# A gated mix of a 2-D FFT filter and a token MLP: 64-row matmul pairs for the odd residues' odd wavenumbers, and filter rows loaded among w2's tiles

## The chip, the cores and the metric

One core of one Trainium2 chip. The metric is the time of one execution on the device in microseconds; the median of several runs is taken.

## The reference, cut to what matters

```python
def _A_ref(x, w_r, w_i):                       # x: 1 x 2048 x 512, w: 2048 x 257
    X = rfft2(x.astype(float32), axes=(-2, -1))
    X = X * (w_r + 1j * w_i)
    return irfft2(X, s=(2048, 512), axes=(-2, -1)).astype(bfloat16)

def _B_ref(x, w1, b1, w2, b2):                 # w1: 2048 x 1792, w2: 1792 x 2048
    h = _layernorm(x, axis=-1)
    u = gelu(einsum("bsd,sf->bdf", h, w1) + b1)
    return (einsum("bdf,fs->bds", u, w2) + b2).transpose(0, 2, 1)

x = A_x
g = sigmoid((x * gate_w).sum(-1, keepdims=True))
return g * _A_ref(x, A_w_r, A_w_i) + (1 - g) * _B_ref(x, B_w1, B_b1, B_w2, B_b2)
```

All inputs are bfloat16. Branch A filters x with a 2-D Fourier transform; branch B is an MLP over the 2048 tokens; a gate per token mixes the two.

## The kernel before, in words

The 2048 tokens are read as 16 tiles `j` of 128 tokens, in four residues `r` modulo 4 and four quarters `q`. Residues are called even or odd below by `r`.

**Branch B** is matmuls of 128x128 weights on 512 columns. The first product (line L716) accumulates 16 token tiles into each of 14 feature tiles `ft`; ScalarE applies the gelu (L732) into `gl`. The second (L1065) accumulates the 14 feature tiles into each of the 16 token tiles; ScalarE scales and adds the bias (L1071). The weights of both products go through the same SBUF buffers: `wa` holds feature tiles 0 to 6, two `wb` buffers the rest, first w1's, then, when TensorE has done with them, w2's.

**Branch A** runs beside it, in stages:
- a radix-4 split over the quarters on VectorE (`q4a`, `q4b`), a DFT over tokens on TensorE (L565 to L568, table `ta`), evacuated by ScalarE (L571), and a second split (`d2`, `radix4`: L596 to L609). The spectrum lies in two halves `lt`: even wavenumbers (0) and odd ones (1). `sp0` and `sp1` (L621 to L639) repair one special column with twelve operations of a few elements;
- a DFT over the 512 channels (L664), evacuated by ScalarE (L671), recombined by `tb2` (L680 to L682, with twelve edge operations L686 to L688 in all) into `B`;
- the filter: a butterfly (`bfly`, L831, L832), products with the filter's real and imaginary part (`mul`, L839), their combination (`comb`, L844, L845) and a second butterfly (`ob`, L851 to L853), for `lt` 0 and then 1. Beside it stand the repairs of the first and last channel wavenumber, `wprep`, `c0a`, `c0b`, `c0c`, and of the Nyquist row, `nyq`, which works on one partition with 512 elements. Nine repaired lines are copied by DMA into `s9` (`lines`), multiplied by a small matrix on TensorE (`linem`, L871), copied out by ScalarE (L873) and written back into `B` by DMA;
- the inverse radix-4 split (`radix4` again) and the inverse DFT over tokens. For even residues it is `i1` (L929 to L934). For the odd residues' even wavenumbers it is `i1s` (L897): the 128 rows of contraction are two halves of 64 that share one table, so two 64-row matmuls run side by side, into banks `fa` and `fb`, and `eo2` (L905) adds and subtracts the halves. For the odd residues' odd wavenumbers it is `i1` with 256 columns (L925), evacuated by L940;
- `zf` and `fq` (L953 to L966), the inverse DFT over channels (`i3`, L1008 to L1012), evacuated with the gate as scale (L1016), then `es`, `es2` and `fin2` (L1042 to L1084) add branch A to branch B's tile. The last tile is finished by `fin` (L1078) in pieces.

**What sets the order.** Nothing is ordered on the chip. `add(engine, duration, emit, reads, writes, prio, ...)` records a task; `Plan.order` walks through a model of the five engines and the DMA with these durations, priorities and buffer counts, and the tasks are emitted in the order that results. Each engine then takes its instructions in that fixed order and waits on semaphores. The model's DMA has one queue, and `late` and `nbytes` of a load are its costs there.

**Loads.** All but a few go through SyncE's queue, in order: x and the first w1 tiles, the tables, the rest of w1, with the filter rows of `A_w_r` (`ld_W(0)`, 16 transfers) ahead of w1's last tiles and those of `A_w_i` (`ld_W(1)`, 16 transfers) behind them, then w2's 14 tiles with the inverse table `ti` and the channel table `tg` ahead of the last three. Filter rows have 257 elements, 514 bytes. SyncE has at most eight transfers under way.

The matmul of the odd residues' odd wavenumbers:

```python
for c in range(2):
    f = (5 - c) * P
    T.matmul(p1[:, v], lhsT=d(c), rhs=ti[:, f:f + L], start=(c == 0), stop=(c == 1))
```

Of the kernel before, what the change touches and what calls it, by code (L numbers as in the profile page):

```python
# [16 lines left out]
P = 128  # L17
# [13 lines left out]
def ti_at(r):  # L31
    return (0, 1024, 512, 1920)[r], (512, 896)[r % 2]


def make_tables():

    p = np.arange(P)
    r4 = np.arange(4)
# [6 lines left out]
    ti = np.zeros((P, 3072))  # L45
    for r in range(4):
# [6 lines left out]
        th = ang(s, 1 + 4 * (p ^ 96), S)  # L53
# [7 lines left out]
        if r % 2:  # L61
            sg = np.where(p < 64, 1.0, -1.0)[:, None]
            th = ang(k, s, S)
            v = v.reshape(P, 7, P)
            v[:, 0] = np.cos(th)
            v[:, 1] = sg * np.cos(th)
            v[:, 2] = -np.sin(th)
            v[:, 3] = -sg * np.sin(th)
            v[0, 2:4] = alt * (0.5 ** 0.5 if r == 1 else -(0.5 ** 0.5))
            th = ang(1 + 4 * (p ^ 96), s, S)  # L70
            v[:, 4] = -np.sin(th)
            v[:, 5] = np.cos(th)
            v[:, 6] = np.sin(th)
            ti[:, o:o + w] = v.reshape(P, w)
        else:
            s5 = np.append(s, 512)
            for lt, kk in enumerate((k, 1 + 4 * (p ^ 96))):
                th = ang(kk, s5, S)
                c, n = np.cos(th), -np.sin(th)
                if lt == 0:  # L80
                    n[0, 0:P] = 0.0 if r == 0 else -alt
                u = v[:, 256 * lt:256 * lt + 256]
                u[:, 0:P], u[:, P:] = c[:, 0:P], n[:, 0:P]
                if r == 0 and lt:
                    u[:, P] = -n[:, P]
                elif r == 0:
                    ti[:, 2816:2879], ti[:, 2943:3007] = n[:, 2:P:2], n[:, 1:P:2]
                    u[:, 0:65], u[:, 66:130] = c[:, 0:129:2], c[:, 1:P:2]
                    u[0, 66:130], ti[0, 2879:2943] = 0.0, 1.0
# [49 lines left out]
class Plan:  # L139
# [33 lines left out]
    def order(self):  # L173
# [17 lines left out]
        while events:  # L191
# [19 lines left out]
            while progress:  # L211
                progress = False
                for eng, ts in pending.items():
# [3 lines left out]
                    for t in ts:  # L217
                        if t.ready <= now + 1e-9 and all(caps[a] > 0 for a in t.alloc):
                            if best is None or key[t] < key[best]:
                                best = t  # L220
# [50 lines left out]
def kernel(  # L271
# [42 lines left out]
    def alloc_first():  # L314
# [15 lines left out]
        t["wn"] = sb([1, 2, WL], BF16, "wn")  # L330
# [3 lines left out]
        t["sp"] = sb([P, 4, 2, 4], F32, "sp")  # L334
# [3 lines left out]
        t["cm"] = sb([P, 4, 4, 2], F32, "cm")  # L338
# [94 lines left out]
    wsrc = (A_w_r, A_w_i)  # L433

    def ld_W(comp):
        v = wsrc[comp].rearrange("(e c k) l -> c e k l", e=4, k=4)
        z = wsrc[comp].rearrange("(v u w) l -> w u v l", v=4, u=2)

        def emit():
            W, u = t["W"][:, comp], t["wt"][:, comp]  # L440
            dma(u[64:127, :, 0:257], v[65:128, :, 0, :])
            dma(u[0:64, :, 0:257], v[64:128, :, 2, :])
            dma(u[127:128, 0:2, 0:257], z[0:1, 1, 2:4, :])
            dma(u[127:128, 3:1:-1, 0:257], z[0:1, 0, 0:4:3, :])
            for e in range(4):
                dma(W[:, 1, e, 1, 0:257], v[:, 3 - e, 3, :].rearrange("(o i) l -> o i l", o=4)[:, ::-1])
            for o in range(4):
                dma(W[32 * o:32 * o + 32, 1, :, 0, 0:257], v[96 - 32 * o:128 - 32 * o, :, 1, :])
            dma(W[1:64, 0, :, 0, 0:257], v[1:64, :, 0, :])
            dma(W[64:128, 0, :, 0, 0:257], v[0:64, :, 2, :])  # L450
            dma(W[0:1, 0, :, 0, 0:257].rearrange("w (u v) l -> w u v l", u=2), z[0:1, :, 0:2, :])
            dma(t["wn"][:, comp, 0:257], wsrc[comp][1024:1025, :])
        return emit

    for comp in range(2):
        add("SP", 12.3, ld_W(comp), writes=[("W", comp), ("wt", comp)], prio=17 + 8 * comp, nbytes=300000, after=[a0])
        if comp == 0:
            load_wb(1)

    def ld_ti():  # L460
        t["ti"] = sb([P, 3072], BF16, "rot")
        dma(t["ti"][:], tabs["ti"])
# [157 lines left out]
    def sp0():  # L620
        V.tensor_copy(t["sp"][:], t["X"][:, 0, :, :, :, 0])  # L621
    dk = [("D", r) for r in range(4)]
    add("DVE", tiny(1), sp0, reads=dk, writes=["sp"], prio=0)

    def sp1():
        sp, sd, fx = t["sp"], t["sd"], t["fx"]
# [7 lines left out]
        V.tensor_scalar_mul(sd[:, 0, 0, 1], sd[:, 1, 1, 1], c)  # L634
        V.tensor_scalar_mul(sd[:, 1, 0, 1], sd[:, 0, 1, 1], -c)
        V.tensor_add(fx[:, 1, 0], sp[:, 0, 1], sd[:, 0, 0, 1])
        V.tensor_sub(fx[:, 3, 0], sp[:, 0, 1], sd[:, 0, 0, 1])
        V.tensor_sub(fx[:, 1, 1], sd[:, 1, 0, 1], sp[:, 2, 1])
        V.tensor_add(fx[:, 3, 1], sd[:, 1, 0, 1], sp[:, 2, 1])  # L639
    add("DVE", tiny(12), sp1, reads=["sp"], writes=["fx"], prio=0)  # L640

    for lt in (0, 1):
# [3 lines left out]
               dk + ([] if lt else ["sp"]), [("Z", lt, 0), ("Z", lt, 1)], pr, False)  # L646
# [9 lines left out]
    for lt in (0, 1):  # L656
        for e in (0, 2, 1, 3):
# [16 lines left out]

            if e >= 2:
                def tb2(lt=lt, e0=e - 2):
# [6 lines left out]
                    if e0:  # L683
                        for i in range(2):
                            bh, vh = b[:, i::2], v[:, 2 * i:2 * i + 2]
                            V.tensor_sub(bh[:, :, 1:3, 0], vh[:, :, 0, 0:4:3, 0], vh[:, :, 1, 0:4:3, 0])  # L686
                            V.tensor_copy(bh[:, :, 0:4:3, P], vh[:, :, 0, 1:3, 0])
                            V.tensor_copy(bh[:, :, 1:3, P], vh[:, :, 1, 1:3, 0])  # L688
                es_ = (e - 2, e) if e == 2 else (0, 1, 2, 3)
                add("DVE", tt(1024) + 2 * tt(508) + tiny(6) * (e > 2), tb2, reads=[("R", lt, i, c) for i in (e - 2, e) for c in range(2)],  # L690
                    writes=[("B", lt, i) for i in es_], prio=2.5)


# [61 lines left out]
    add("DVE", 0.4, omg, reads=["b2h"], writes=["g", "omg"], prio=0)  # L755


    add("SP", 0.2, ld_ti, writes=["ti"], prio=39, nbytes=754176, after=[pl.last_w["pa", r, dq] for r in range(4) for dq in range(4)])
# [32 lines left out]
    add("DVE", 0.4, wprep, reads=[], writes=[("W", 0), ("W", 1), "wpm"] + wtk, prio=1)  # L791


    for lt in range(2):
# [3 lines left out]
        def c0a(lt=lt):  # L798
            b, c0 = t["B"][:, lt], t["c0"][:, lt]
            V.tensor_copy(c0[:, :, 0, :], b[:, :, 0:2, 0])  # L800
            V.tensor_copy(c0[:, :, 1, :], b[:, :, 3:1:-1, 0])
        add("DVE", 0.2, c0a, reads=bk, writes=[("c0", lt)], prio=0)
        if lt == 0:
            def nyq():
                pz = sb([1, 1280], F32, "X")
                na = pz[:, 0:1024].rearrange("p (i v l) -> p i v l", i=2, v=2)
                nn = t["nn"] = pz[:, 1024:1280].bitcast(BF16).rearrange("p (v l) -> p v l", v=2)
                wn, v = t["wn"], t["B"][0:1, 0, 0, 2:4, :]
                for i in range(2):
# [3 lines left out]
                V.tensor_mul(pz[:, 0:2], t["c0"][0:1, 0, 0, 1, :], wn[:, 0, 0:257:256])  # L813
                V.tensor_add(nn[:, 0, 0:1], pz[:, 0:1], pz[:, 1:2])
                V.tensor_sub(nn[:, 1, 0:1], pz[:, 0:1], pz[:, 1:2])
            add("DVE", 3 * d1(512) + 0.35, nyq, reads=[("B", i, e) for i in range(2) for e in range(4)] + [("W", 0), ("W", 1), ("c0", 0)] + pbk, writes=["nn"], prio=0.5)

        def c0b(lt=lt):
            c0, cm, ce, pm = t["c0"][:, lt], t["cm"], t["ce"][:, lt], t["wpm"]
            V.tensor_mul(cm[:, 0], c0[:, :, 0], pm[:, 0, lt])  # L820
            V.tensor_mul(cm[:, 1], c0[:, :, 1], pm[:, 1, lt])
            V.tensor_mul(cm[:, 2], c0[:, :, 0], pm[:, 1, lt])
            V.tensor_mul(cm[:, 3], c0[:, :, 1], pm[:, 0, lt])
            V.tensor_sub(ce[:, :, 0], cm[:, 0], cm[:, 1])
            V.tensor_add(ce[:, :, 1], cm[:, 2], cm[:, 3])
        add("DVE", tiny(6), c0b, reads=[("c0", lt), "wpm"], writes=[("ce", lt)], prio=0.3)
# [7 lines left out]
        for comp in range(2):  # L834
# [5 lines left out]
            add("DVE", tt(4096), mul, reads=["xs", ("W", comp), ("W~", comp, lt)], writes=[("pp", "st")[comp]], prio=pr)  # L840
# [45 lines left out]
    i1t = {}  # L886
    for rs, h in ((0, 0), (0, 1), (1, 0), (1, 1)):
        if rs:
            def i1s(h=h):
                p2 = t["i1s", h] = [ps([P, 2, 2, P], F32, tag, 2) for tag in ("fa", "fb")]  # L890
# [242 lines left out]
```

## Time and profile before

| | before |
|---|---|
| median of 3 runs, us (lowest to highest) | 126.42 (126.18 to 126.42) |
| the profiled execution's own time, us | 126.11 |
| its span, us | 124.3 |
| granted TensorE clock | 1.000 |
| TensorE busy, us | 119.8 |
| VectorE busy, us | 113.2 |
| ScalarE busy, us | 83.7 |
| bytes moved by DMA, MB | 23.10 |

The span runs from the first to the last instruction; some 1.8 us of the execution's time lie around it. Busy time of TensorE is modelled from pipelined matmuls, so starts are a better guide than durations: a matmul listed with 0.38 us may be followed by the next 0.22 us later.

### The profile page before, as it was taken

Reading aid. Unit: us, or ns where it says so; the run is one execution under the profiler, and the core shown is the slowest. Engines: PE = TensorE matmul, PEld = TensorE weight load, DVE = VectorE, ACT = ScalarE, POOL = GpSimd, SP = SyncE. Lnnn points to the kernel's source line nnn. Section 1 sums busy time; section 2 is a strip of 40 time slices with the busy share of each in tenths; the row PEclk is TensorE's granted clock in tenths of the full one; section 3 lists DMA queues with packets and bytes.
Section 4 is the critical chain, followed back from the end, with each engine's and each line's share of the span. In section 5 each row is a group of like instructions: output and inputs, shape, how many; then the busy total and the mean of one; then the engine's idle time right before and its main releaser. Section 6 shows DMA issues by size and latency. Waiting matters only on the chain.

```text
span 124.3 us, 2226 instructions
## 1 busy us (share of the span) xinstructions
PE 119.8 (96%) x789; PEld 67.7 (54%) x789; DVE 113.2 (91%) x271; ACT 83.7 (67%) x176; POOL 0.2 (0%) x4
## 2 busy tenths in 40 slices
PE   7799999999999999999999999999999999999990
PEld 2245555555645466644445555555577576665590
DVE  1789999999999999999999999999969999999951
ACT  3696889699999999999520003742279999993200
POOL 0000000000000000000000000000000000000000
PEclk9999999999999999999999999999999999999999
DMA  3999999992459946699999930000000000003751
GB/s 112 316 329 306 397 394 385 376 300 62 112 121 258 289 97 121 157 395 406 420 414 415 422 132 0 0 5 0 3 0 0 5 0 0 0 12 131 287 211 42
DMA packets 18203, 23.10 MB, mean 186 GB/s; under 512 B 2174, under 2 KB 15888, under 8 KB 18192
## 3 DMA queue, kind: packets, MB, share of 16 engines
q1 hardware_dynamic: 17616, 22.34, 52.9%
q10 hardware_dynamic: 576, 0.62, 1.6%
q8 instruction: 6, 0.10, 0.3%
q14 instruction: 5, 0.04, 0.1%
HBM read 20.84 MB, written 2.10 MB: 185 GB/s over the span
## 4 chain that ended last, share of the span: by engine, by line
PE 93%; DMA 2%; DVE 1%; ACT 0%; issue 0%
PE acc L1065 33%; PE acc L716 31%; PE fb L716 6%; PE fb L1065 6%; PE fa L716 3%; DMA x<-in_A_x_dram 2%; PE fb L664 1%; PE fa L664 1%; PE fa L565 1%; PE fa L566 1%; PE fa L897 1%; PE fb L1012 1%; PE fa L1012 1%; PE fa L568 1%; PE fa L567 1%; PE fb L925 1%
## 5 line engine op out<-in xcount | busy, mean ns | idle before, releaser
L716 PE MATMUL acc<-h,wb 128*128 128x512 bf16 x112 | 27.0, 379 | 0.0
L1065 PE MATMUL acc<-gl,wb 128*128 128x512 bf16 (+1 forms) x98 | 24.7, 372 | 0.0
L1065 PE MATMUL acc<-gl,wa 128*128 128x512 bf16 (+1 forms) x98 | 24.0, 371 | 0.0
L1071 ACT ACTIVATE x<-acc,ombb,omg 128x512 bf16<-128x512 f32 x12 | 9.0, 780 | 19.3 <-PE acc L1065 19.3
L1065 PEld LDWEIGHTS <-wa 128*128 128x128 bf16 x126 | 13.4, 113 | 9.6
L1065 PEld LDWEIGHTS <-wb 128*128 128x128 bf16 x126 | 13.2, 114 | 9.4
L716 PE MATMUL acc<-h,wa 128*128 128x512 bf16 x64 | 17.1, 379 | 0.0
L716 PEld LDWEIGHTS <-wb 128*128 128x128 bf16 x112 | 10.7, 98 | 10.3
L716 PEld LDWEIGHTS <-wa 128*128 128x128 bf16 x112 | 10.3, 98 | 10.9 <-DMA wa<-in_B_w_dram 1.1
L489 DVE BATCH_NORM_STATS2 stats<-x 128x6 f32<-128x512 bf16 x12 | 8.1, 676 | 2.1 <-DMA x<-in_A_x_dram 2.1
L746 ACT ACTIVATE x<-x 128x512 bf16<-128x512 bf16 x16 | 10.0, 654 | 0.0
L571 ACT CAST xp<-fa 128x512 bf16<-128x512 f32 x16 | 9.0, 594 | 1.5 <-PE fa L568 1.4
L716 PE MATMUL fb<-h,wa 128*128 128x512 bf16 x32 | 9.9, 379 | 0.0
L732 ACT ACTIVATE gl<-acc,b1f 128x512 bf16<-128x512 f32 x11 | 7.8, 711 | 2.8 <-PE acc L716 2.8
L537 ACT ACTIVATE h<-x,nmr,rstd 128x512 bf16<-128x512 bf16 x11 | 8.4, 806 | 1.3 <-DVE nmr L528 1.1
L716 PE MATMUL fa<-h,wa 128*128 128x512 bf16 x16 | 6.1, 378 | 0.9 <-DVE h L531 0.9
L664 PEld LDWEIGHTS <-X 128*128 128x128 bf16 x64 | 4.7, 98 | 2.2
L1016 ACT ACTIVATE B<-fb,g 128x512 bf16<-128x512 f32 x8 | 5.5, 689 | 0.0
L1016 ACT ACTIVATE B<-fa,g 128x512 bf16<-128x512 f32 x8 | 5.5, 685 | 0.0
L671 ACT CAST X<-fb 128x512 bf16<-128x512 f32 x8 | 5.1, 639 | 0.0
L671 ACT CAST X<-fa 128x512 bf16<-128x512 f32 x8 | 5.1, 635 | 0.0
L741 DVE TENSOR_TENSOR x<-x,gw 128x2048 bf16<-128x2048 bf16 x4 | 4.7, 1214 | 0.0
(183 smaller groups left out, 234.8 us busy)
## 6 DMA issues: line engine op xcount, KB each, us to landing
wb<-in_B_w_dram SPq DMA_DIRECT2D x11, 512.0 KB
wa<-in_B_w_dram SPq DMA_DIRECT2D x7, 512.0 KB
wa<-in_B_w_dram SPq DMA_DIRECT2D x2, 896.0 KB
wb<-in_B_w_dram SPq DMA_DIRECT2D x4, 384.0 KB
out_dram<-x SPq DMA_DIRECT2D x3, 512.0 KB
x<-in_A_x_dram SPq DMA_DIRECT2D x2, 512.0 KB
wa<-in_B_w_dram SPq DMA_DIRECT2D x4, 224.0 KB
rot<-dft_ti SPq DMA_DIRECT2D x1, 768.0 KB
```

The lines of the kernel that those rows point to most:

```text
L489: V.bn_stats(out=t["stats"][:, j, :], in_=t["x"][:, j // 4, j % 4, :])
L537: add("ACT", 0.71, lambda j=j: A.activation(t["h"][:, j // 4, j % 4, :], t["x"][:, j // 4, j % 4, :], ActF.Identity, bias=t["nmr"][:, j:j ...
L571: add("ACT", act(512), lambda r=r, dq=dq: A.copy(xe(r)[:, :, :, dq, :], t["pa", r, dq][:]), reads=[("pa", r, dq)], writes=[("X", r, dq)], ...
L664: T.matmul(pb[:, k % 2, k // 2], lhsT=t["X"][:, lt, EX[e], c, k, :], rhs=tbl(k, c), start=True, stop=True)
L671: A.copy(t["X"][:, lt, EX[e]].rearrange("p c j l -> p (c j l)").rearrange("p (h c g b) -> p h c g b", h=2, c=2, b=2)[:, :, c], t["pb", lt, ...
L716: T.matmul(t["u", ft][:], lhsT=w[:, j // 4, j % 4, c * P:(c + 1) * P], rhs=t["h"][:, j // 4, j % 4, :], start=(j == jorder[0]), stop=(j == ...
L732: gelus.append(add("ACT", act(512, 1) , lambda ft=ft: A.activation(t["gl"][:, ft, :], t["u", ft][:], ActF.Gelu_apprx_tanh, bias=t["b1f"][: ...
L741: add("DVE", tt(2048), lambda r=r: V.tensor_mul(t["x"][:, :, r, :], t["x"][:, :, r, :], t["gw"][:, None, :].to_broadcast([P, 4, D])), read ...
L746: A.activation(t["x"][:, q, r, :], t["x"][:, q, r, :], ActF.Copy, accum_out=t["glog"][:, 4 * q + r:4 * q + r + 1])
L1016: A.activation(eo_v(p)[:, n].rearrange("p h (n w) -> p h n w", w=2), t["i3", j][:].rearrange("p h (w n) -> p h n w", w=2), ActF.Copy, scal ...
L1065: T.matmul(t["y", j, m][:, cs], lhsT=w[:, o, 512 * q + r:512 * q + 512:4], rhs=t["gl"][:, ft, cs], start=(ft == 0), stop=(ft == NFT - 1))
L1071: A.activation(tbuf(j).rearrange("p h d -> p (h d)"), t["y", j, 0][:], ActF.Identity, bias=t["ombb2"][:, j:j + 1], scale=t["omg"][:, j:j + 1])
```

## The change

It has three parts.

**The odd residues' odd wavenumbers.** The order of the odd wavenumbers over the 128 partitions changes (`sig`), so that partition p and p + 64 hold wavenumbers that share a table up to signs. `i1s` now does both halves of the spectrum for the odd residues, as pairs of 64-row matmuls of 128 columns; the 256-column `i1` for odd residues is gone. The two channel parities `h` of one half stand behind each other. `eo2` has a second form for `lt` 1, with an addition, a subtraction in place and two half-size operations. The inverse table shrinks from 3072 to 2112 columns. A factor of the square root of two for 64 partitions is taken into the table and the gate.

**VectorE's small operations.** `sp0` is gone and `sp1` has ten operations; the edge operations of `tb2` work on both residue pairs at once, and the copies among them for `lt` 1 go to ScalarE (`tb2c`); `c0a` goes to ScalarE; `c0b` does both halves in six operations; two of `omg`'s three operations go to ScalarE (`omga`, with a third one for the gate's factor); `zf` has one copy instead of two. `nyq` works on 16 partitions with 16 elements: ScalarE's queue spreads the Nyquist line over them by two DMAs (`nspread`), and two DMAs instead of one bring the result to `s9`. `wprep` and `c0b` move behind the second half's butterfly and among its products.

**Filter rows.** `ld_W` keeps the rows of the first half of the spectrum, and for `A_w_r` the reversed rows of the second half; both stand ahead of w1's last tiles now. The second half's other rows, four reversed transfers of `A_w_i` (`turned`) and two straight ones for each part (`straight`, before four), become loads of their own among w2's tiles 3 to 6 and behind them. The table `ti` and `tg` come behind w2's last tile.

The core of the diff:

```diff
-            v[:, 4] = -np.sin(th)
-            v[:, 5] = np.cos(th)
-            v[:, 6] = np.sin(th)
+            th = ang(1 + 4 * sig, s[0:64], S)
+            v[:, 256:320], v[:, 320:384], v[:, 384:448] = -np.sin(th), np.cos(th), np.sin(th)
...
+    add("SP", 11.5, ld_W(0), writes=[("W", 0), ("wt", 0)] + [("Wl", 0, e) for e in range(4)], prio=17, nbytes=900000, after=[a0], late=1.0)
+    add("SP", 6.0, ld_W(1), writes=[("W", 1), ("wt", 1)], prio=18, nbytes=300000, after=[a0], late=5.0)
+    load_wb(1)
+    for e in range(4):
+        add("SP", 0.6, lambda e=e: turned(1, e), writes=[("Wl", 1, e)], prio=(32.25, 33.25, 34.3, 34.31)[e], nbytes=720000, after=[a0, wa_free])
     for comp in range(2):
-        add("SP", 12.3, ld_W(comp), writes=[("W", comp), ("wt", comp)], prio=17 + 8 * comp, nbytes=300000, after=[a0])
-        if comp == 0:
-            load_wb(1)
+        add("SP", 1.2, lambda comp=comp: straight(comp), writes=[("Wl", comp, 4)], prio=33.5 + 0.5 * comp, nbytes=360000, after=[a0, wa_free])
...
+    add("ACT", 0.45, tb2c, reads=[("R", 1, i, c) for i in range(4) for c in range(2)], writes=[("B", 1, i) for i in range(4)], prio=4.4)
...
     def omg():
-        V.tensor_scalar(t["omg"][:], t["g"][:], -0.5, 0.5, op0=Alu.mult, op1=Alu.add)
-        V.tensor_scalar(t["g"][:], t["g"][:], 0.5, 0.5, op0=Alu.mult, op1=Alu.add)
         V.tensor_mul(t["ombb2"][:], t["omg"][:], t["b2h"][:].rearrange("p q r -> p (q r)"))
+    def omga():
+        A.activation(t["omg"][:], t["g"][:], ActF.Copy, bias=0.5, scale=-0.5)
+        A.activation(t["g"][:], t["g"][:], ActF.Copy, bias=0.5, scale=0.5)
+        A.activation(t["g"][64:P, 1:NJ:2], t["g"][64:P, 1:NJ:2], ActF.Copy, scale=0.5 ** 0.5)
...
+            def nspread():
+                for v in range(2):
+                    dma(t["vs"][:, v], t["B"][0:1, 0, 0, 2 + v, :].rearrange("p (a b) -> p a b", b=16), A)
...
-                for i in range(2):
-                    V.tensor_mul(na[:, i], v, wn[:, i, None, 0:L].to_broadcast([1, 2, L]))
+                V.tensor_mul(na[:], t["vs"][:, None].to_broadcast([16, 2, 2, 16]), wn[:, :, None, 0:16].to_broadcast([16, 2, 2, 16]))
...
-                dma(t["s9"][8:9], t["nn"].rearrange("p v l -> p (v l)"))
+                for v in range(2):
+                    dma(t["s9"][8:9, L * v:L * v + L].rearrange("p (a b) -> p a b", b=16), t["nn"][:, v])
...
+                            f = (320 - 64 * c) if lt else c * P
                             for m in range(2):
                                 k = slice(64 * m, 64 * m + 64)
-                                T.matmul(p2[m][:, n, v], lhsT=t["B"][k, 0, r, 2 * c + v, h:L:2], rhs=ti[k, 2 * c * P:2 * c * P + P], start=(c == 0), stop=(c == 1))
+                                T.matmul(p2[m][:, n, v], lhsT=t["B"][k, lt, r, 2 * c + v, h:L:2], rhs=ti[k, f:f + P], start=(c == 0), stop=(c == 1))
...
+                zv = t["zz"][:, 1, h, 1].rearrange("p v k r a -> p r (v k) a")
+                x = lambda u: u.rearrange("p r v (k a) -> p r (v k) a", k=2)
+                V.tensor_add(zv[:, :, :, 0:64], x(e), x(o))
+                V.tensor_sub(e, e, o)
+                V.tensor_sub(zv[:, :, 0:4:2, 64:P], x(e)[:, :, 0:4:2], x(e)[:, :, 1:4:2])
+                V.tensor_add(zv[:, :, 1:4:2, 64:P], x(e)[:, :, 0:4:2], x(e)[:, :, 1:4:2])
...
-                        if r % 2:
-                            for c in range(2):
-                                f = (5 - c) * P
-                                T.matmul(p1[:, v], lhsT=d(c), rhs=ti[:, f:f + L], start=(c == 0), stop=(c == 1))
```

More of the change, by code (lines that the diff above doesn't have):

```diff
@@ L217, in order @@
                     for t in ts:
-                        if t.ready <= now + 1e-9 and all(caps[a] > 0 for a in t.alloc):
+                        if t.ready <= now + 1e-9 and all(caps[a] >= t.alloc.count(a) for a in t.alloc):
                             if best is None or key[t] < key[best]:
@@ L790, in wprep @@
         V.tensor_sub(pv[1], ends[1][:, :, 0], ends[1][:, :, 1])
-    add("DVE", 0.4, wprep, reads=[], writes=[("W", 0), ("W", 1), "wpm"] + wtk, prio=1)
+    add("DVE", 0.2, wprep, reads=[("W", 0), ("W", 1)] + wtk + [("Wl", comp, e) for comp in range(2) for e in range(5)], writes=["wpm"], prio=1)
     for lt in range(2):
@@ L796, with c0a @@
         bk = [("B", lt, e) for e in range(4)]
[L798 to L802, printed above, removed]
-        if lt == 0:
-            def nyq():
[L805 to L809, printed above, removed]
-                    V.tensor_mul(na[:, i], v, wn[:, i, None, 0:L].to_broadcast([1, 2, L]))
+        if lt == 0:
+            def c0a():
+                b, c0 = t["B"], t["c0"]
+                A.copy(c0[:, :, :, 0, :], b[:, :, :, 0:2, 0])
+                A.copy(c0[:, :, :, 1, :], b[:, :, :, 3:1:-1, 0])
+            add("ACT", 0.45, c0a, reads=[("B", i, e) for i in range(2) for e in range(4)], writes=[("c0", i) for i in range(2)], prio=4.5)
@@ new lines @@
+        if lt == 0:
+            def nspread():
+                for v in range(2):
+                    dma(t["vs"][:, v], t["B"][0:1, 0, 0, 2 + v, :].rearrange("p (a b) -> p a b", b=16), A)
+            b0 = [("B", 0, e) for e in range(4)]
+            add("DMA", 3.5, lambda: None, reads=b0, writes=["vs"], after=[add("ACT", 0.12, nspread, reads=b0, prio=2)])
+            def nyq():
+                na, nn, wn, e = t["na"], t["nn"], t["wn"], t["na"][0:1, 0, 0, 0:2]
+                V.tensor_mul(na[:], t["vs"][:, None].to_broadcast([16, 2, 2, 16]), wn[:, :, None, 0:16].to_broadcast([16, 2, 2, 16]))
@@ L818, in c0b @@
[L818 to L826, printed above, removed]
+                V.tensor_mul(e, t["c0"][0:1, 0, 0, 1, :], wn[0:1, 0, 0:17:16])
@@ L828, in bfly @@
+        if lt == 0:
+            add("DVE", tiny(6), c0b, reads=[("c0", 0), ("c0", 1), "wpm"], writes=[("ce", 0), ("ce", 1)], prio=3.22)
         def bfly(lt=lt):
@@ L839, in mul @@
                 V.tensor_mul(o, xs, w)
-            add("DVE", tt(4096), mul, reads=["xs", ("W", comp), ("W~", comp, lt)], writes=[("pp", "st")[comp]], prio=pr)
+            add("DVE", tt(4096), mul, reads=["xs"] + ([("Wl", comp, e) for e in range(5)] if lt else [("W", comp), ("W~", comp, 0)]), writes=[("pp", "st")[comp]], prio=pr)
         def comb(lt=lt):
@@ L946 @@
-                add("ACT", act(512), i1ev, reads=[("i1", h, r, lt)] + pbk, writes=[("zz" if r % 2 else "ze", h, r, lt)], prio=1.7, free=[tag], after=[lined])
+                        u = ti[:, 256 * lt:256 * lt + 256]
+                        if r == 0 and lt == 0:
+                            T.matmul(p1[:, v, 65:256], lhsT=d(1), rhs=t["ti"][:, 1920:2111], start=True, stop=False)
+                            T.matmul(p1[:, v, 128:192], lhsT=d(0), rhs=u[:, 66:130], start=False, stop=True)
+                            T.matmul(p1[:, v, 0:65], lhsT=d(0), rhs=u[:, 0:65], start=True, stop=True)
+                        else:
+                            T.matmul(p1[:, v, P:], lhsT=d(1), rhs=u[:, P:], start=True, stop=True)
+                            T.matmul(p1[:, v, 0:P], lhsT=d(0), rhs=u[:, 0:P], start=True, stop=True)
@@ L948 @@
+                add("ACT", act(512), i1ev, reads=[("i1", h, r, lt)] + pbk, writes=[("ze", h, r, lt)], prio=1.7, free=[tag], after=[lined])
             if r % 2 == 0:
@@ L959, in zf @@
                         V.tensor_sub(k1[:, :, :, ::-1], e[:, :, :, 0:P], e[:, :, :, P:L])
-                add("DVE", 2 * tt(512) + (tiny(2) if r == 0 else 0), zf, reads=[("ze", h, r, lt) for lt in range(2)], writes=[("zz", h, r, lt) for lt in range(2)], prio=3.55)
+                add("DVE", 2 * tt(512) + (tiny(1) if r == 0 else 0), zf, reads=[("ze", h, r, lt) for lt in range(2)], writes=[("zz", h, r, lt) for lt in range(2)], prio=3.55)
         def fq(rs=rs, h=h):
```

198 lines of the change are left out of this document (105 added, 93 removed).

## The prediction

> **What bounds the kernel now.** I read the page's first two parts, then the chain of waits, then the timelines of TensorE, VectorE and the DMA issues around the changed steps, then the windows table for DMA.
>
> ```profile
> PE 119.8 (96%) x789; PEld 67.7 (54%) x789; DVE 113.2 (91%) x271; ACT 83.7 (67%) x176; POOL 0.2 (0%) x4
> ...
> PE 93%; DMA 2%; DVE 1%; ACT 0%; issue 0%
> ```
>
> TensorE carries 93% of the chain that ends last. In its timeline the only gaps after the first real matmul (5.29 us) are the ends of the 64-row blocks below. A microsecond of matmul removed is a microsecond of time, as long as nothing makes TensorE wait. VectorE, at 91%, has little room: what it feeds must arrive before TensorE's fixed order gets there. The tail shows who waits for whom (the bracket is idle time before, and its releaser):
>
> ```profile
> 118.41 0.75 DVE L1078 SCALAR_TENSOR_TENSOR x<-acc,omg,x 128x512 bf16<-128x512 f32 x1 [0.23 <-PE acc L1065]
> 119.94 0.48 DVE L1078 SCALAR_TENSOR_TENSOR x<-acc,omg,x 128x256 bf16<-128x256 f32 x1 [0.78 <-PE acc L1065]
> ```
>
> VectorE waits for TensorE here, so VectorE's thinning alone buys nothing.
>
> **Part 1: the odd residues' odd wavenumbers (TensorE).** Removed: four L925 groups of four matmuls. Added: two more of the L897 blocks, each 8 pairs of 64-row matmuls.
>
> ```profile
> 95.70 0.60 PE L925 MATMUL fb<-rot,B 128*128 128x256 bf16 x4
> 96.14 0.59 PE L1065 MATMUL acc<-gl,wb 128*128 128x512 bf16 x2
> 96.66 0.23 PE L897 MATMUL fa<-rot,B 64*128 64x128 bf16 x1
> 96.67 0.23 PE L897 MATMUL fb<-rot,B 64*128 64x128 bf16 x1
> ...
> 97.06 0.22 PE L897 MATMUL fa<-rot,B 64*128 64x128 bf16 x1
> 97.07 0.22 PE L897 MATMUL fb<-rot,B 64*128 64x128 bf16 x1
> 97.22 0.62 PE L1065 MATMUL acc<-gl,wb 128*128 128x512 bf16 x2
> 97.77 0.23 PE L897 MATMUL fa<-rot,B 64*128 64x128 bf16 x1
> ```
>
> From start to start, an L925 group takes 96.14 - 95.70 = 0.44: four are 1.76. A 512-column matmul takes 0.216 (x15 in 3.24 in the chain). From 96.14 to 97.22 lie two of them and one block: 1.08 - 0.43 = 0.65 per block, 1.30 for the two. Inside, both halves of a pair start 0.01 apart, and seven steps take 97.06 - 96.66 = 0.40, so a pair costs 0.057; the rest, 0.65 - 8 x 0.057 = 0.19, is paid once for entering and leaving the 64-row shape. So the stage is 1.76 + 1.30 = 3.06 now. In the changed program's order the two h-blocks of one half of the spectrum stand back to back, so there are again two entries: 2 x (16 x 0.057 + 0.19) = 2.20. The sum is **-0.86**. If the joined blocks paid 0.19 each, four entries would leave 2.58, -0.48.
>
> The Trainium skill ("TensorE: Matmul & The Clock Gate", Measured speedup vs the span model) has four row tiles reach 3.07 times, not 4. By that share a pair would cost 0.057 x 4/3.07 = 0.074 and the new stage 2.75, a gain of 0.31. The trace's pairs of this very shape decide.
>
> Evacuation: four ScalarE copies (L940, 0.47 apart) become four copies of the same size. VectorE gains `eo2` for this half, twice: a strided add as L905 (0.75 for two, 0.37), a plain subtraction as L577 (0.33) and two 256-element ones, between L859 (0.09 step) and L681 (0.33), taken as 0.20: 1.1 each, **+2.2 on VectorE**, after the last filter product.
>
> **Part 2: VectorE's small operations.** They run 0.07 to 0.10 apart. Up to the butterfly (L831, 53.02): the copy `sp` and two of the twelve steps of `sp1` go (36.96 to 38.18 is 1.22 now, ten steps make about 0.8: -0.42), and three edge operations of `tb2` (-0.21). L680 at 51.60 waits for ScalarE, which has one gate pass (0.61) fewer ahead, so of this 0.60 arrives. Two `c0a` copies move: -0.14. From there to the first filter product (L839, 61.15): five edge operations, -0.36, and all that stands from 57.00 to 61.15, `wprep`, `c0a`, twelve `c0b` steps, `nyq` (58.36 to 60.79) and `omg`: -4.15. The product starts near 61.15 - 5.25 = 55.9. Behind the two products (4.4) now come `nyq` on 16 partitions (six operations between 0.1 and 0.15 plus two dependency gaps like 60.46 to 60.64: 0.7; if it kept its 2.43, +1.7), the combination (2.4), one `omg` operation, `ob` (2.35), the second butterfly (2.38), `wprep` (0.2), two products with six `c0b` between (5.0) and only then `c0c`: 73.45, where it is at 70.41 now. The written rows of the first half then end (L612, now 86.94) at 73.65 + 9.45 = 83.1, the second half's first pair (L602, now 90.84) at 87.0, its second pair (now 92.05) at 88.2.
>
> TensorE hides all of this if its order allows. There the first of these matmuls stands behind 103 output matmuls instead of 123: 63.56 + 103 x 0.216 + 0.216 = 86.0 (now 90.32). The second half's first is asked for at 87.4, its second pair at 88.75. The margins are **0.4 and 0.5**, where the trace now has 91.76 - 90.92 = 0.84 and 0.95. Beyond them VectorE's lateness is TensorE's idle time, one to one. `fq` of the first half is needed at 96.1 and ready near 94, the second at 101.6 and near 100. At the end VectorE is some 2 us early.
>
> **Part 3: ScalarE.** It gains two copies for `tb2c`, two for `c0a` (L1025 like, 0.12 apart), three for `omga` (L748: 0.21 each), two DMA issues (its store: 0.35), in all about 1.9. They stand between 53 and 63, where it now idles 2.77 at 63.76. New waits of VectorE: `omg` waits for `omga`, ready near 62.9, wanted at 63.4; behind it stands the whole spectrum chain. `nyq` waits for the spread line, issued near 53, wanted at 60.3.
>
> **Part 4: DMA.**
>
> ```profile
> 44.00:46.00 2.00, 2.00 (x26) 1.53 (x25) 1.97 (x3) 2.00 (x7) 0.00 (x0) 1.00 0.46 98
> ...
> 58.00:60.00 2.00, 2.00 (x11) 0.93 (x10) 1.97 (x9) 1.98 (x8) 0.00 (x0) 1.00 1.02 414
> ...
> 74.00:76.00 2.00, 2.00 (x11) 1.05 (x10) 2.00 (x2) 0.00 (x0) 0.00 (x0) 1.00 0.00 0
> ```
>
> Last columns: DMA share and GB/s. Filter rows alone run at 98 GB/s, w2 at 414. Eight row transfers (0.79 MB) move behind the third w2 tile, so w1's last tiles issue near 40 (now 36, read from 53.4) and w2 starts near 43 (now 50.70, less twelve issues of 0.35 to 0.6 and the waits among them). Seven tiles at 1.27 and the rows at 98 to 414 GB/s (8 to 1.9) end at 54 to 60, with what SP waits for the spread line (to 56) by 61. VectorE first reads the rows at 68.2. The next w2 tiles wait for TensorE (63.7) as now and are all in by 70, first read at 70.0 and 75. Cost **nothing**; the cover is 7 us. The first DFT table shrinks from 0.77 to 0.53 MB, read at 86: nothing. Of the lines behind `c0c`, three transfers issue instead of two, behind everything else on SP:
>
> ```profile
> 70.74 0.74 SPq L312 DMA_DIRECT2D s<-B  x1
> 71.53 0.57 SPq L312 DMA_DIRECT2D s<-X  x1
> 87.09 0.68 SPq L312 DMA_DIRECT2D B<-s  x1
> ```
>
> 73.75 + 0.74 + 2 x 0.57 + gaps = 75.7 for the last issue. B<-s has its last packet at 88.59, 0.82 after its issue ended: landing 76.5 with an idle queue (as at 74 to 76 above); s<-X, in a busy one, 1.75 after: 77.5. TensorE asks at 63.56 + 64 x 0.216 = 77.4 (now 80.82). I take 76.5, no wait.
>
> **Sum.** -0.86 on TensorE, nothing else on the path. Profiled execution 126.11 - 0.86 = 125.25; the median 126.42 stands 0.31 above that execution, giving 125.56, rounded **125.6**.
>
> **Rivals.**
> 1. The nine lines land late. For it: three small transfers in a row, and `c0c` 3 us later against an asking time 3.4 earlier. Late by 0.1 (busy queue) to 0.4: TensorE stands, gain 0.46 to 0.76, 125.7 to 126.0. The Trainium skill ("DMA: Bandwidth & Descriptors", Anatomy of one DMA) gives about 2.0 us fixed cost, nearly all write receipt, for its software path; 75.7 + 2.0 = 77.7 would cost 0.3. The trace's 0.82 speaks against it. Chance 0.12.
> 2. Pairs gain less: four entries, -0.48: 125.9; or halves that do not overlap, 16 x 0.057 more: 126.4, no change. The 0.01 between starts speaks against. Chance 0.07.
> 3. Slower: VectorE comes late to the second half's matmuls. TensorE's order asks 4 us sooner; my working leaves 0.4. Each microsecond beyond is lost: above 0.4 + 0.86 = 1.26 late the kernel is slower, above 1.5 visibly. Its likeliest source is `nyq`: at its old 2.43, so 1.7 late, it gives -0.86 + 1.3 = +0.44, 126.9. For it: thin margins, and a wait of its own for the spread line. Against it: its operations handle 16 to 64 elements a row, and the chain's long operations are as they were. Chance 0.17.
>
> **Chances.** Forecast 0.64, rivals 0.12, 0.07, 0.17. About 0.2% (0.25 us) can be told from no change. Faster: 0.64 + 0.12 and most of rival 2's first case, about 0.75; same: 0.09, with rival 3's small lateness; slower 0.16. The range reaches from 125.2 (another 0.3 from the scatter seen between runs, 126.11 to 126.42) to 126.5 (0.9 of waiting), leaving out the rest of rival 3 and the far edge below.
>
> **What would show it.** Two double blocks of 1.1 each and no gap around them; no idle TensorE before the line matmul (near 77.4) and before the matmuls at 86 to 89; the first filter product near 56; `c0c` near 73.5; DMA quiet from 70 on. A TensorE gap over 0.4 at any of these places makes the prediction wrong; so does a pair step above 0.06.

## The result and the profile after

| | before | after |
|---|---|---|
| median of 6 runs, us (lowest to highest) | 126.27 (126.02 to 126.42) | 130.75 (128.75 to 131.54) |
| the profiled execution, us | 126.11 | 128.75 |
| its span, us | 124.3 | 127.0 |
| TensorE busy, us | 119.8 | 118.7 |
| VectorE busy, us | 113.2 | 112.0 |

The change makes the kernel slower: ratio 1.0276, 95% interval 1.0206 to 1.0347. The forecast was 125.6. Three of the six executions (130.85 to 131.54) show a mean granted clock of 0.987 instead of 1.000, and the ratio leaves them out; the other three have a median of 129.81. The profiled execution is the shortest of the six, so what follows accounts for 2.7 us of the 3.5 between 129.81 and 126.27; what the longer ones add is not shown, because no trace of them was taken.

The page of after, busy time and the chain of waits by engine:

```profile
PE 118.7 (93%) x791; PEld 66.8 (53%) x805; DVE 112.0 (88%) x253; ACT 85.3 (67%) x183; POOL 0.2 (0%) x4
...
PE 65%; DMA 22%; SPq 6%; DVE 4%; issue 1%; ACTq 0%
```

TensorE and VectorE, which the change meant to unload, are less busy. But TensorE carries 65% of the chain instead of 93%, and DMA has 22% where it had 2%. The waits of after, by engine and line, with what they waited for (total, times, longest):

```profile
PE fa L898 <- DMA s<-nn: 2.5, 1, 2.5
...
DVE wpm L812 <- DMA W<-in_A_w_i_dram: 1.1, 1, 1.1
...
PE acc L1097 <- DMA wa<-in_B_w_dram: 0.6, 1, 0.6
```

L898 is the line matmul, L812 the first reader of the late filter rows, L1097 the second product. From one matmul's start to the next, less the 0.216 of a matmul, TensorE loses 2.62 before L898 (78.01 to 80.85) and 0.80 at the w2 tile (64.88 to 65.90). The chain of after in order of time shows where that comes from:

```profile
49.68 10.94 DMA W<-in_A_w_i_dram
60.61 0.02 issue
60.63 0.33 SPq L307
...
61.59 8.07 DMA W<-in_A_w_i_dram
69.66 0.02 issue
69.68 0.19 DVE wpm L812
69.87 2.20 DVE xp L865
...
76.51 4.20 DMA s<-nn
80.71 0.14 issue
80.85 0.38 PE fa L898
```

Two of the four late transfers of reversed rows (66 KB each) take 10.94 and 8.07 us from issue to landing. I had them all landed by 61. The next w2 tile is issued at 60.63, 0.02 us after the first of the two has landed. The windows of after (last columns: DMA share and GB/s) say that these were no busy microseconds:

```profile
60.00:62.00 2.00, 2.00 (x11) 0.90 (x10) 1.83 (x8) 2.00 (x6) 0.00 (x0) 1.00 0.64 132
62.00:64.00 2.00, 2.00 (x11) 0.93 (x9) 2.00 (x4) 1.37 (x7) 0.00 (x0) 1.00 0.76 241
64.00:66.00 2.00, 1.36 (x7) 0.56 (x6) 2.00 (x3) 0.47 (x1) 0.00 (x0) 1.00 0.14 47
...
76.00:78.00 2.00, 2.00 (x11) 1.02 (x9) 1.97 (x3) 0.00 (x0) 0.00 (x0) 1.00 0.92 360
78.00:80.00 2.00, 0.39 (x2) 0.00 (x0) 2.00 (x3) 0.00 (x0) 0.00 (x0) 1.00 0.15 52
```

At 64 to 66, while TensorE waits for a w2 tile, 0.14 of 16 engines, about two, are at work, at 47 GB/s. And w2, predicted to be in by 70, still flows at 76 to 78, so the nine lines queue behind it. SyncE's timeline of after shows the queue blocked at the same place: seven w2 tiles take 6.65 us to issue, the first of them alone 3.42.

```profile
61.01 1.11 SPq L307 DMA_DIRECT2D W<-in_A_w_i_dram  x2
62.22 6.65 SPq L307 DMA_DIRECT2D wb<-in_B_w_dram  x7
69.67 0.33 SPq L307 DMA_DIRECT2D rot<-dft_ti  x1
70.84 0.32 SPq L307 DMA_DIRECT2D tg<-dft_tg  x1
75.04 0.74 SPq L307 DMA_DIRECT2D s<-B  x1
```

**Theory 1.** The new `turned` reads two runs of 64 reversed rows; before, four runs of 32. A transfer has landed when its semaphore has got 16 increments. For one of these the records show one entry right after the issue (47.76) and two 7 us later (54.47, 54.88), so the first must stand for 14; before, it stands for 12, and four follow. By theory 1 a transfer is spread over as many engines as it has runs. Two engines carry all reversed rows, every w2 tile's share on these two waits behind them, and with eight transfers under way SyncE can issue nothing for the other fourteen. The first w2 tile behind the last of these rows fits: 14 of its increments have come by 68.68, the last two come at 70.30 and 70.82. The Trainium skill has theory 1's rule ("DMA: Bandwidth & Descriptors", Why a DMA increments its semaphore by 16 and not by 1): the engines are the largest number up to 16 that divides the slowest dimension of both patterns, the lowest-numbered ones, and the sequencer writes the other increments itself; the 14 and 2, and the 12 and 4, agree; which engines they are no run here shows.

**Theory 2.** Rows of 514 bytes among w2's tiles slow the stream, however many engines carry them. **Theory 3.** The tables `ti` and `tg`, now behind w2, stand ahead of the nine lines.

### The profile page after: what moved, and what is told of

It is laid out like the page before. It is cut to its first block, busy times and chain, and to the rows that moved or that the text cites. A ratio compares the mean times of both kernels' runs of the same rounds, so it can differ in the third digit from the quotient of the medians.

```text
span 127.0 us, 2239 instructions
## 1 busy us (share of the span) xinstructions
PE 118.7 (93%) x791; PEld 66.8 (53%) x805; DVE 112.0 (88%) x253; ACT 85.3 (67%) x183; POOL 0.2 (0%) x4
## 4 chain that ended last, share of the span: by engine, by line
PE 65%; DMA 22%; SPq 6%; DVE 4%; issue 1%; ACTq 0%
PE acc L1097 24%; PE acc L734 17%; DMA W<-in_A_w_i_dram 15%; SPq L307 6%; PE fb L734 5%; DMA s<-nn 3%; DMA wa<-in_B_w_dram 3%; PE fa L734 3%; PE fb L1097 3%; DVE st L865 2%; DVE xp L865 2%; PE fa L934 1%; PE fa L575 1%; PE fa L576 1%; PE fb L1044 1%
## 5 line engine op out<-in xcount | busy, mean ns | idle before, releaser
L734 PE MATMUL acc<-h,wb 128*128 128x512 bf16 x108 | 26.3, 379 | 0.1
L1097 PE MATMUL acc<-gl,wb 128*128 128x512 bf16 (+1 forms) x93 | 23.4, 371 | 0.3 <-issue 0.2
L1097 PE MATMUL acc<-gl,wa 128*128 128x512 bf16 (+1 forms) x97 | 22.9, 372 | 0.7 <-DMA wa<-in_B_w_dram 0.6
L1097 PEld LDWEIGHTS <-wa 128*128 128x128 bf16 x126 | 13.2, 114 | 10.9 <-DMA wa<-in_B_w_dram 1.1
L1097 PEld LDWEIGHTS <-wb 128*128 128x128 bf16 x126 | 13.0, 113 | 9.1 <-DMA wb<-in_B_w_dram 0.4
L734 PE MATMUL acc<-h,wa 128*128 128x512 bf16 x62 | 16.6, 379 | 0.1
L900 ACT CAST s<-fa 32x512 bf16<-32x512 f32 x1 | 0.6, 577 | 16.8 <-PE fa L898 16.8
```

The costliest lines, as they stand in the source:

```text
L734: T.matmul(t["u", ft][:], lhsT=w[:, j // 4, j % 4, c * P:(c + 1) * P], rhs=t["h"][:, j // 4, j % 4, :], start=(j == jorder[0]), stop=(j == ...
L1097: T.matmul(t["y", j, m][:, cs], lhsT=w[:, o, 512 * q + r:512 * q + 512:4], rhs=t["gl"][:, ft, cs], start=(ft == 0), stop=(ft == NFT - 1))
```

## The experiments

The kernel before had medians of 126.15 to 126.21 beside these runs.

### Reversed rows on 16 engines

```diff
-    ...rearrange("(e i h k) l -> k e h i l", e=4, h=2, k=4)[3, 3 - e][:, ::-1])
+    ...rearrange("(e c k) l -> k e c l", e=4, k=4)[3, 3 - e])
```

> The changed kernel with one edit: the four late transfers of reversed rows of the filter's imaginary part read the same 128 rows unreversed, in one plain pattern of 128 rows, at the same place in the queue, with the same bytes and row size (the second half's filter rows are in another order, so its products are left wrong; all work stays). In the changed kernel each of these transfers has two runs of 64 reversed rows, and its completions come 14 at once and the last two 5 to 8 us later. Theory 1 (two DMA engines carry the reversed rows and every later w2 tile's share waits on those two): the spread removes the backlog: no wait at the filter rows (1.06 on VectorE), none at the w2 tile (0.80 on TensorE), and the line matmul's 2.62 goes; 128.75 - 0.8 - 2.6 = 125.3 for the profiled execution, 125.1 to 125.8. Theory 2 (small rows among the w2 tiles slow the stream however many engines carry them): as the changed kernel, 128.5 or more. Theory 3 (the tables stand in the queue ahead of the nine lines): the filter rows' wait goes and part of the line wait stays, 126.5 or more.

The rows land in another order here, with the same bytes and the same work. One thing in this text is wrong: all eight transfers use the function, so the four early ones were spread too, and w2's first tile was issued at 42.7 instead of 44.4. Measured: 125.70, ratio 0.9959 (0.9946 to 0.9972). All three waits are gone; the chain by engine:

```profile
PE 92%; DMA 2%; DVE 1%; issue 1%; ACT 0%
```

The semaphore of such a transfer now gets 16 increments spread over time. From 129.81 to 125.70, 4.1 us come back from one access pattern (3.0 between the two profiled executions): theory 1, and nothing of theories 2 and 3 is needed for the size of the loss.

### Only the four late ones on 16 engines

```diff
+    ... (the plain pattern if comp else the reversed one)
```

> In the run with 16-way row reads, all eight transfers of reversed rows were spread, the four early ones of the real part as well, since both use the same function, and w2's first tile was issued 2.4 us earlier than in the changed kernel. Here the four early ones keep their two runs of 64 reversed rows and only the four late ones, among w2's tiles, read 128 rows unreversed (the second half's imaginary filter rows are in another order, all work stays). Theory 1 as stated (the late four are what the stream waits on): recovery to 125.6 to 126.0, no wait at the filter rows, the w2 tile and the line matmul. Rival 1b (it was the early four, which push w2's start back): most of the loss stays, 127.5 or more.

Measured: 125.73, ratio 0.9969 (0.9936 to 1.0002). w2's first tile is issued at 44.48 as in after, and still no wait is left. For the filter rows and the lines it is the late four. Its windows while rows and w2's tiles are mixed:

```profile
56.00:58.00 2.00, 2.00 (x11) 0.88 (x9) 2.00 (x4) 2.00 (x7) 0.00 (x0) 1.00 0.44 102
58.00:60.00 2.00, 2.00 (x11) 0.88 (x9) 2.00 (x2) 2.00 (x10) 0.00 (x0) 1.00 0.97 295
60.00:62.00 2.00, 1.95 (x10) 0.93 (x10) 1.83 (x8) 2.00 (x7) 0.00 (x0) 1.00 0.75 167
```

Even here the engines idle at times. Two of them lag: of the increments of w2's first tile the third last comes at 50.68, the last two at 52.32 and 52.95, and only eight transfers may be under way. The early four still have two runs here; with them spread as well one increment lags (50.79, the one before at 49.39). Why that one does was not tried. Beside after, everything from the last reversed row on is 3.8 us earlier: that row (65.84 against 69.66), w2's last tile (74.75 against 78.58), the tables' end (76.43 against 80.19). The w2 tile for which TensorE waited in after, the seventh, is only 0.43 earlier (65.42 against 65.85); there is no wait because TensorE comes for it 0.5 later than in after (65.61). With the early four spread too, it lands at 62.97. So for this wait the early four count as well.

### Four runs instead of two

```diff
+    ...rearrange("(e o i k) l -> k e o i l", e=4, o=4, k=4)[3, 3 - e][:, ::-1])
```

> The same four transfers cut into four reversed runs of 32 rows instead of two of 64, same place, bytes and row size (again the rows of the second half's imaginary part are in another order, all work stays). Theory 1: each engine carries 32 rows instead of 64, so the backlog of a transfer is halved: 126.0 to 127.2, the line matmul's wait 0.5 to 1.5. Theory 2: no difference from the changed kernel, 128.5 or more.

Measured: 125.9, ratio 0.9968 (0.995 to 0.9987), 12 increments at once and four later. All eight transfers are cut so, and their rows stay reversed: it is the number of runs that costs, not the direction. The time is better than theory 1 had said: half the backlog costs not half the time but nothing, since the last reversed rows land at 65.9, before VectorE reads them (L812 at 68.94), and w2's seventh tile lands at 63.64.

### Two runs in the kernel before

```diff
-    dma(W[:, 1, e, 1, 0:257], v[:, 3 - e, 3, :].rearrange("(o i) l -> o i l", o=4)[:, ::-1])
+    dma(W[:, 1, e, 1, 0:257], v[:, 3 - e, 3, :].rearrange("(o i) l -> o i l", o=2)[:, ::-1])
```

> The kernel before with one number changed: its eight transfers of reversed rows are cut into two runs of 64 rows instead of four of 32, in their old place (rows land in another order, all work stays). Theory 1: each transfer holds two engines for about 1.8 us instead of four for 0.9; eight of them push w2's first tile from 50.7 to 55 to 58, and its first half, asked for at 63.6 to 65, lands up to 3 us late: 127 to 129. Theory 2 (only rows mixed among w2's tiles hurt): the time of before, 126.2.

Measured: 128.39 in the profiled execution, 130.9 to 132.5 in the three others; there is no ratio. The place is the old one, no w2 tile runs beside the rows, and the number alone costs 2.2 us in the shortest of the four. w2's first tile is issued at 54.92 (before: 50.70), and TensorE waits twice:

```profile
PEld L1065 <- DMA wa<-in_B_w_dram: 2.5, 2, 1.4
...
PE acc L1065 <- DMA wa<-in_B_w_dram: 1.7, 2, 0.9
```

### The late rows ahead of w2

The six late loads stand in front of w2's first tile.

```diff
+    order_ = [q for q in order_ if q not in rows_late]
+    at = order_.index(w2_first)
+    order_ = order_[:at] + rows_late + order_[at:]
```

> The changed kernel with the six late row loads moved ahead of the first w2 tile in the DMA queue; the pattern is untouched, so the output is the same. Theory 1: the reversed rows still need two engines for some 4 x 6 us and the w2 tiles behind them wait on the same two; they start only some 2.4 us earlier, so 1 to 2 of the 2.6 stay: 126.5 to 128. Theory 2 (mixing small rows into the stream): the mix is gone, 125.3 to 125.8. Theory 3: no change at the lines, 128 or more.

Measured: 131.95, ratio 1.0446 (1.0405 to 1.0487): theory 2 wanted a recovery, and theory 1's number was too low as well. With nothing beside them, SyncE takes 1.65 to 2.31 us to issue a transfer behind a two-run one, where others take some 0.6; w2 starts at 55.65 instead of 44.4. The windows while only reversed rows move:

```profile
50.00:52.00 2.00, 1.95 (x22) 1.41 (x22) 1.68 (x8) 2.00 (x5) 0.00 (x0) 1.00 0.17 44
52.00:54.00 2.00, 2.00 (x14) 1.12 (x13) 2.00 (x5) 1.30 (x3) 0.00 (x0) 1.00 0.15 38
```

0.15 to 0.17 of 16 engines is 2.4 to 2.7, at about 40 GB/s: the price by itself. In after, w2's tiles at least used the fourteen others.

### The lines ahead of the tables

`ti` and `tg` are issued behind the nine lines, in the same way.

> The changed kernel with the tables ti and tg moved behind the nine lines in the queue, nothing else. Theory 3 (the tables ahead of the nine lines make them late): the lines land as soon as issued, near 76.5, and the whole 2.6 goes: 126.1. Theory 1: the two engines' backlog of w2 tiles (last packets at 77.9) is still ahead of the lines, so only the tables' share of about 1.4 goes: 127.2 to 127.6, with 1.0 to 1.5 of the line wait left, plus the 0.8 at the w2 tile.

Measured: 127.51, ratio 1.0108 (1.0066 to 1.015). The line wait falls from 2.62 to 1.05, the w2 wait stays (0.90):

```profile
DVE wpm L812 <- DMA W<-in_A_w_i_dram: 1.2, 1, 1.2
PE fa L898 <- DMA s<-nn: 0.9, 1, 0.9
PE acc L1097 <- DMA wa<-in_B_w_dram: 0.7, 1, 0.7
```

Theory 3 is a part of the line wait, not its cause: the backlog is there without the tables.

### The late rows through GpSimd's queue

```diff
+    nc.gpsimd.tensor_copy(t["pw8"][:], t["wt"][:, 1, 0, 0:8])     # once, ahead of the first
-    dma(..., ...[:, ::-1])
+    dma(..., ...[:, ::-1], nc.gpsimd if comp else None)
```

> The changed kernel with the four late transfers of reversed rows issued from GpSimd's queue instead of SyncE's, held back there by a copy of eight elements that waits for the filter rows loaded before (near 44); the pattern stays two runs of 64 rows, the output is the same, the other engines' orders too. Theory 1: two DMA engines per transfer remain, but SyncE no longer stalls behind them and its eight transfers under way are w2 tiles: the stream runs at 350 to 414 GB/s and the three waits go, if GpSimd's transfers use other engines than the lowest two or start early enough: 125.5 to 126.2. If they use the same two engines and hold w2's shares up there, half the loss stays: 127 to 128. Theory 2 (small rows beside w2 tiles slow the stream, whoever issues them): 128.5 or more.

Measured: 128.53, ratio 1.0186 (1.0155 to 1.0216), the number that theory 2 gave. The trace says otherwise than either theory: these transfers are on all 16 engines (16 increments spread over 3 us, eight rows to a packet of 4112 bytes), but they run beside w1's last and w2's first tiles, and all together moves at 230 to 243 GB/s there (after: 280 to 413):

```profile
46.00:48.00 2.00, 1.95 (x25) 1.41 (x24) 2.00 (x5) 2.00 (x5) 0.24 (x1) 1.00 1.01 243
48.00:50.00 2.00, 2.00 (x22) 1.29 (x20) 1.88 (x4) 1.93 (x5) 0.00 (x0) 1.00 1.17 231
```

w2's seventh tile lands at 67.56, 2.0 us after TensorE wants it. So sharing costs time as well, which theory 1 had left out; the two-engine pattern is not the only way to lose this cover. From 58 to 66, with the straight rows among w2's tiles, the windows show 203 to 211 GB/s again, and how much of the 2.0 belongs to which rows was not separated. The Trainium skill's same section has an exception for some software transfers (those of GpSimd's queue), all 16 engines with a sixteenth of the partitions each: eight rows of 514 bytes are these 4112.

### All eight early through GpSimd's queue

> The changed kernel with all eight transfers of reversed rows issued from GpSimd's queue, held back by one small copy until the first filter rows have landed (near 31), so that they run from 32 to 42 us, where SyncE's rows leave the DMA engines half idle; the output is the same, the order on the other engines too. In the run with four of them on GpSimd's queue these transfers were spread over all engines in packets of 4112 bytes, and what they cost was w2's speed beside them (230 GB/s at 46 to 52 us). Theory 1 with this addition: SyncE's queue is rid of all two-engine transfers, w2 starts 2 to 4 us earlier and nothing runs beside it but the straight rows: no wait at the filter rows, at the w2 tiles and at the line matmul: 125.2 to 125.9. Rival (rows among w2's tiles cost their time whoever carries them; here the straight rows still do): a wait at w2's tiles of 0.5 to 2 stays, 126.5 to 128.5.

> The same with the tables ti and tg moved behind the nine lines in SyncE's queue. If the stream has caught up (theory 1) this changes nothing: 125.2 to 125.9, the same as with all eight on GpSimd's queue. If the stream is still late, it saves up to 1.4 at the line matmul against that run.

Measured: 128.3 for both, ratios 1.0142 (1.011 to 1.0174) and 1.0132 (1.0107 to 1.0158). The w2 wait is gone or small (0 and 0.47) and the queue is empty by 76.3, and yet the line matmul waits 2.1 and 2.05. The second run shows that no table is in the way. ScalarE's timeline of the first shows what is:

```profile
55.54 0.51 ACTq L307 DMA_DIRECT2D vs<-B  x1
56.09 0.59 ACT L794 CAST W<-fa 128x512 bf16<-128x512 f32 x1 [2.19 <-DMA wa<-in_B_w_dram]
```

The spread line's second transfer (`vs`) waits for a w2 tile that used its completion semaphore before, ScalarE stands behind it, and it lands at 63.5; VectorE's `nyq`, ready at 61.4, waits 2.25:

```profile
63.61 0.21 DVE L835 TENSOR_TENSOR na<-vs,wn 16x64 f32<-16x64 bf16 x1 [2.25 <-issue]
```

### The same with the spread line in that queue

```diff
-    dma(t["vs"][:, v], t["B"][0:1, 0, 0, 2 + v, :].rearrange(...), A)
+    dma(t["vs"][:, v], t["B"][0:1, 0, 0, 2 + v, :].rearrange(...), nc.gpsimd)
```

> All eight transfers of reversed rows on GpSimd's queue, and behind them, in the same queue, the two transfers that spread the Nyquist line, which ScalarE's queue issued till now. With the eight alone the line matmul still waited 2.1 us, and the trace puts that on the spread line: its second transfer was issued at 55.5, because ScalarE waited 2.2 us for the completion lane it shares with a w2 tile, and landed at 63.5, 2.25 us after VectorE wanted it. If that is the whole of what was left, both land near 59, nyq waits for nothing and the line matmul neither: 125.2 to 125.9. Rival (the straight rows beside w2's tiles hold the spread line up on the engines themselves, whichever queue issues it): it lands at 60 to 62, half a microsecond to two of waiting stay, 126.3 to 127.8.

Measured: 126.03, ratio 0.9993 (0.9967 to 1.0019). The spread lands at 56.1 and 56.8, no wait of TensorE over 0.4 is left after its start, and with the change's own data 3.8 us against after are back (129.81 to 126.03). That is as far as it went: with the rows in another order the change was 0.3 to 0.4% faster than the kernel before (in one of three such runs the interval touches 1); with its own rows no version was, by more than the interval.

### The late four early, without and with the spread line

> Only the four late transfers of reversed rows on GpSimd's queue, as in the first run of that kind, but held back by the first filter rows (near 31) instead of those of the imaginary part (near 43): they run at 32 to 40 us, beside the filter rows, not beside w1's last tiles and w2's first. Theory 1: w2's stream is as with 16-way late rows (w2's first tile issued near 44.5), all waits gone but the start's: 125.5 to 126.1. Rival (the four software transfers cost the same 4 us of stream wherever they stand): 127.5 to 128.6 as when they ran at 43 to 56.

> The same four transfers early on GpSimd's queue, and the two spread transfers of the Nyquist line there too, behind them. If the spread line was not late in the run with the four alone, no difference from it, 125.5 to 126.1; if it was, this run is faster by what VectorE waited for it, up to 2 us.

Measured: 127.72 and 127.75, ratios 1.0111 (1.0079 to 1.0144) and 1.0138 (1.0089 to 1.0187). The first waits 1.7 for a w2 tile (landed 67.0): its software rows, at 36 to 45, held up the imaginary part's other rows (landed by 46.5, in after by 43.2), and w2 started at 47.3. The second has no wait over 0.25 after 14 us; its profiled run lost 1.6 us in the first eight matmuls, which ran 0.43 apart instead of 0.22. So this pair doesn't tell what the spread line is worth here, and that stays open.

## Why the prediction was wrong, step by step

**Part 4 failed, and with it everything.** "Cost nothing; the cover is 7 us" rested on a stream whose rows and first seven w2 tiles are in by 61 and which is quiet from 70 on. In after it ends at 80.19, some 10 us later, and two errors stand in that. The run with the late four on 16 engines splits them: there it ends at 76.43. So 6.4 us are my sum: I divided each stream's bytes by its rate alone, but mixed they ran at 102 to 295 GB/s, and w2's last tile landed at 74.75 instead of 70; the tables, which the change itself puts behind w2, take another 1.7, and I had left their time out. That alone would have cost nothing, since the lines land at 77.4 in any case; it used the cover up. The other 3.8 us are the access pattern, which I had not priced at all, and it came through: 2.6 at the lines and, with the early rows, 0.8 at a w2 tile. The page of before had the clue. I took its 98 GB/s of filter rows as a rate, and the same line showed a DMA share of 0.46 with a full queue: why does half of it idle? The diff had the rest, `h=2` where `o=4` had been.

**Rival 1 was the right place with the wrong size.** The nine lines did land late, by 2.6 and not 0.1 to 0.4. Its sum is tight even without the backlog: in the run with 16-engine rows the last line is issued at 75.70, as predicted, but lands at 77.40, 1.12 after its issue ends where I took 0.82, and TensorE asks at about 77.6. My 0.9 of room was 0.2 at most. The 0.82 was read from the last packet of `B<-s`; the last increment of that transfer came at 89.04, 1.27 after its issue had ended. In after the last line lands 3.62 after its issue has ended (77.09 to 80.71). With 1.12 it would have landed at 78.2, when TensorE asks there, so by this sum the wait is the queue's backlog and not VectorE's lateness.

**Part 1 held.** Pairs step at 0.056 (95.01 to 95.79 in 14 steps; predicted 0.057), and a double block takes 1.10, as predicted:

```profile
97.48 0.38 PE L1097 MATMUL acc<-gl,wa 128*128 128x512 bf16 x1
97.80 0.23 PE L934 MATMUL fa<-rot,B 64*128 64x128 bf16 x1
```

The next L1097 matmul starts at 98.80: 1.32 less one matmul of 0.22. The first double block took 1.34, 0.24 more, of which 0.18 are put down to "issue". So -0.62 of the -0.86 on these lines. With 16-engine rows, from TensorE's first real matmul to the end of the span, the kernel takes 118.2 (123.9 - 5.7) against 119.0 (124.3 - 5.3): -0.8. That the profiled execution itself is only 0.4 below that of before (125.72 against 126.11) is that first matmul: 5.68 there, 5.29 in before, since x's first tile landed 0.4 later. Whether the change has a part in that stays open; after itself had 5.35.

**Part 2 held.** First product 56.00 (55.9); `c0c` 74.74 (73.45), of which 1.06 are the wait for the rows and 0.23 `nyq`, which took 0.93 (60.40 to 61.33) and not 0.7. Rival 3, VectorE late, didn't come: its chain was late only where DMA made it so.

**Part 3 held, narrowly.** ScalarE's `omga` ended at 63.28 (62.9), the spread line landed at 57.6 and 59.9, wanted at 60.4. The run with eight transfers on GpSimd's queue shows what hung on this: 2.2 us, by a semaphore shared with w2's tiles.

The sum for after: -0.62 + 0.80 + 2.62 = +2.80, and the spans differ by 2.7.

## What to carry to other kernels

In this kernel a transfer's time went by its bytes over the engines that carried it, so read the slowest dimension of each new access pattern before pricing it, and take a DMA share well below 1 with a full queue as a sign that few engines carry it. Moving such a transfer among large ones made them wait here, because each large one has a share on the same engines and the queue holds only eight. A cover found by adding up rates needs the rates of the mix, not those of each stream alone.

## What the hardware showed that was not expected

- Transfers with two runs left some 14 of 16 engines idle (47 GB/s at 64 to 66 in after; 38 to 44 from 50 to 54 with the late rows ahead of w2), and SyncE's issue of the next one stretched from 0.6 to 1.65 to 2.31 us.
- Stalls one after the other were followed by a lower granted clock, which cost time beside them. With the late rows ahead of w2, five waits of 0.6 to 0.9 follow each other from 64 to 70, and then the windows show, in the column behind POOL's (granted clock):

```profile
68.00:70.00 2.00, 0.75 (x3) 0.15 (x2) 1.34 (x3) 1.68 (x7) 0.00 (x0) 0.93 1.04 406
70.00:72.00 2.00, 1.75 (x5) 0.65 (x6) 1.97 (x3) 0.00 (x0) 0.00 (x0) 0.50 1.02 414
72.00:74.00 2.00, 2.00 (x8) 0.83 (x7) 2.00 (x5) 0.00 (x0) 0.00 (x0) 0.71 1.04 422
```

  Matmuls there start up to 0.43 apart instead of 0.22: the 21 from 70.25 to 76.20 take 5.95 us where 21 x 0.216 are 4.54, so 1.4 us beside the 4 of the stalls. One trace shows this.
